# Another stored order of the same tasks in a one-core attention and gated-MLP kernel

## The chip, the cores and the metric

One core of a Trainium2 chip runs the whole program. The metric is the device time of one execution in microseconds (us). Engines are named as in the profile: PE (TensorE; PEld is its weight load), DVE (VectorE), ACT (ScalarE), POOL (GpSimd), SP (SyncE, which issues all DMAs here).

## The reference

For 8 batches of 576 positions, 8 heads of 64 each:

```python
q_d, k_d, v_d = means of q, k, v over groups of 4 positions
out_d = softmax(q_d k_d^T / 8) v_d                  # 144 positions, repeated 4 times
out_l = softmax(q k^T / 8, only |i-j| < 4) v        # a band of 7
x = out_up + out_l                                  # heads side by side: 576 x 512
h = gelu_tanh(x @ w_in)                             # 512 -> 1024
u, v = halves of h; v_n = layernorm(v) * g_ln
gated = u * (w_sg @ v_n + b_sg)                     # w_sg: 576 x 576 over positions
return x + gated @ w_out
```

## The kernel before, in words

Heads are worked on in pairs: 8 batches of 4 pairs give g = 0 to 31. Everything is cut into 2,432 named tasks of one to some thirty instructions. For a pair g: `lq`, `lk`, `lv`, `lw` load it (SP); `qs`, `ks`, `vs` sum groups of four positions; `S` and `Y` are the scores of the band and of the pooled keys (PE; one task `YS` from g = 4 on); `mx`, `my` take row maxima, `ia`, `ib` subtract them (g under 4), `ma`, `mb` add the mask instead (g from 4); `ea`, `eb`, `ec` are the exponentials (ACT), `es`, `re`, `rc` the sums and reciprocals, `np`, `nq` the normalizations; `T`, `U`, `t` turn the probabilities on PE, `pa`, `pb`, `pc`, `pe` copy them out of PSUM; `D` multiplies with v (PE); `oe`, `od`, `xa`, `xb` merge both outputs into x.

For a batch b, `v b.s` (5 blocks of positions) and `u b.i` are the two halves of x @ w_in, with GELU in `vg`, `ua` and the layer norm in `vb`, `vp`, `vn`; `s` multiplies with w_sg, `o` with w_out, `oa` adds the result to x, and `os` stores it. From batch 1 on, matrices are split into a high and a low part and multiplied in three passes (`vh`, `vl`, `gh`, `gl` split; from batch 1 or 2 on, `s` and `o` use seven products in place of eight, whose sums are `fa` to `fd` and `ga` to `gd`). In batch 0, `v` is cut finer: `vk s.k` needs x of pair k alone (s is the block of positions) and one block of weights, y k. The weights come as 64-bit words: `w` loads, `wq`, `wu`, `wb`, `wt` make a float of the two words (`wt`, on POOL, comes last), `wh`, `wl` split it.

The order is written out: the string `ORDER` (line 91) holds all tasks in one row, some with an engine behind a slash (`/V` DVE, `/A` ACT, `/P` POOL; without one, the first engine that the task's `add` names). `place` (line 68) reads it: it gives each task its buffers, first freed first used, out of 8 PSUM banks (`ps`), 10 tiles `X` and 38 tiles `R`. The main loop emits tasks in this row, so each engine's queue is the row cut down to its own tasks, and an engine starts a task only after the one ahead of it in its queue. In front of `S0` and `S3`, PE runs 28 and 20 matmuls on zeros (line 1471). SP has at most 6 loads under way (`DEPTH`).

The lines that are spoken of: 608 (`ks`, `qs` on DVE), 611 and 612 (the same on POOL), 674 (`mx`), 713 (`ia`, `ib`), 686 and 688 (`my`), 720 (`es`), 737 (`rc`), 733 (`re` on DVE), 652 (`ma`, `mb`), 418 and 420 (`wb`), 428 (`wt`), 740 and 748 (`np`, `nq` on POOL), 751 and 760 (`T`, `U`, `t`), 812 and 828 (`D`), 665 and 644 (`Y`, `S`), 795, 799 and 835 (`oe`, `od`, `xa`, `xb`), 936 (`vk`, `v` of batch 0), 1250 and 1262 (`ga` to `gd`, `gl`), 1279 (`o`), 1286 (`oa`).

```python
    for word in ORDER.split():
        name, _, e = word.partition("/")
        t = named.pop(name)
        for k in t.takes:
            where[k] = free[k[0]].pop(0)
```

Of the kernel before, what the change touches and what calls it, by code (L numbers as in the profile page):

```python
# [92 lines left out]
qs2/P wuy0 rc0 np0 ib1 S2 mx2 Y2 my2 ea1 ia2 lq3 lk3 ny1 S3 ec1 qs3/P es1 re1 ks3/P nq0/A rc1 np1 ib2 ea2 lq4 qs4/P wy2
lv0 T0 wqy2 ks4 t0 wby0 pa0 U0 Y3 mx3 ia3 ny2 ec2 pb0/V es2 nq1 U1 pc0 pe0 lw0 ib3 ea3 T1 my3 t1 pa1 pb1/V pc1 wty0
re2/V rc2 nq2 ny3/V es3 ec3 pe1 D0 t2 wby2 wz0 oe0 od0 re3 lw1 np2 YS4 wuy2 wty2 wuz0 rc3 nq3 xa0 ma4 mb4 xb0 wy1 wuy1
wqy1 mx4 lv1 T2 np3 U2 pa2 pb2/V lv2 D1 lk5 why2 wby1 nx4 eb4 wty1 lq5 wqz0/V U3 T3 pc2 pe2/V my4 oe1 od1 xa1 xb1 vk0.0
vk2.0 why0 ks5 qs5 vs2 pa3 ny4 pb3 ec4 wly0 vk2.1 wz3 pc3 t3 wbz0 YS5 my5 ma5 mb5 wly2 ea4 wuz3 vk0.1 wtz0 wqz3 vk1.0
re4 rc4 np4 ny5 ec5 lw2 D2 mx5 oe2/V whz0 od2 lv3 xa2 vs3 vk3.0 vk3.1 xb2 nx5 wbz3 wtz3 wy3 pe3 wqy3/V wby3 eb5 ea5
vk1.1 vk1.2 T4 wuy3 re5/V rc5 lw3 D3 vk0.2 nq4/A oe3/V U4 wty3 od3 xa3 xb3 lv4 vk2.2 vs4/V v0.0 nq5 np5 pa4 whz3 vg0.0
v0.2 vg0.2 why3 v0.1 lw4 vg0.1 lq6 qs6 pb4/V pc4/V wz1 wqz1/V wbz1 wlz3 t4 pe4 wz2 wuz2 vb0.2/A vk3.2 wly3 lk6 wq0 ks6/P  # L100
vb0.0 vp0.0 wlz0 T5 v0.3 pa5 vg0.3 wuz1 wtz1 wqz2/V wbz2 D4 YS6 ma6 my6 U5 pb5/V pc5/V mb6 mx6 wtz2 wq2 whq2 vk4.0 vk4.1
u0.4 nx6/V oe4 vb0.1/A vp0.1 lw5 whq0 vn0.0 vp0.2 u0.5 whz1 ny6 wlq2/V vn0.1 vh0.1/V wq4 eb6 ec6 vb0.3 lq7 od4 ea6 re6
ua0.4 ua0.5 whq4/V xa4 wr1 vk4.2 v0.4 t5 xb4 vg0.4 qs7 wr2 wqr2/V u0.2 ua0.2 vl0.1/P u0.6 pe5 vn0.2 vh0.0 wlz1 why1
vp0.3 vn0.3 u0.3 ua0.6 rc6 np6 T6 wqr1/V wur2 ua0.3 wlq0 lv5 vs5/V small vh0.3 lk7 wq3 whq3 wbr2 ks7 wlq4 wbr1 D5 lw7
pa6 YS7 nq6 U6 oe5/V lv6 od5 xa5 my7 ma7 lk8 ks8 vs6/V wur1 mb7 vb0.4/A xb5 pb6 ny7 ec7 u0.0 ua0.0 wly1 vl0.0/P vp0.4
mx7 pc6/V wq1 whq1/V vn0.4 lq8 wlq3/V wlq1/V u0.1 lw6 t6 pe6 lk9 ua0.1 vl0.3/P vh0.2 b u0.7 ua0.7 vh0.4/V vl0.2 nx7 eb7
D6 qs8/P YS8 lk10 ea7 ma8 mb8 my8 ny8 mx8 oe6 nx8/V eb8 lq9 ec8 vl0.4/P s0.0 sa0.0 xh5/V s0.2 ks9/P re7/V sm0.0 rc7
np7/V nq7 ea8 re8 s0.1 wtr2 s0.3 lv7 U7 T7 t7 vs7/V sa0.1 sm0.1/P s0.5 od6 xa6 sa0.2 sm0.2/P sa0.3 pa7 pb7 pc7 pe7/V D7
gh0.0/A rc8 xb6 xh6 qs9 YS9 sm0.3/P sa0.5 whz2 oe7/V np8 T8 s0.4 nq8/A whr2 wr0 wur0 wr3 wtr1 wur3 od7 xa7 ma9 mb9 xb7
xh7 sm0.5/P pa8 U8 pb8 gh0.1/A my9 mx9 t8 lq10 ny9 lv8 vs8/V tq1 pc8 ec9 pe8/V ks10 xl6/P whr1/V s0.7 sa0.7 xh4 nx9  # L110
sa0.4 ea9 qs10/P lw8 D8 oe8 wlz2 YS10 ma10 mb10 eb9 re9 my10 xl7 lk11 xl4/P xc4 od8 xl5/P gl0.1 s0.6 tq3 v1.0 sm0.7/P
ks11 wqr0 wqr3/V rc9 nq9 ny10/V ec10 np9/V vg1.0 vb1.0/A xc7/A v1.3 v1.2 T9 lv9 vs9/V xa8 sm0.4/P t9 xb8 gl0.0/V sa0.6
gh0.2 wbr3 U9 lq11 qs11/P xc5 sm0.6/P gh0.3/A vg1.3 pa9 gl0.2 pb9/V pc9 pe9/V wtr3 xc6/A mx10 tq2 nx10 tq4 v1.1 lw9
vg1.1 wlr1 wbr0 vg1.2 D9 YS11 tq0 ma11 wtr0 vp1.0 vb1.1/A mb11 my11 mx11 u1.2 whr3 wlr3/V gl0.3/V vb1.2/A whr0 lk12
vn1.0/A vb1.3/A u1.0 ua1.0 wlr2/V ua1.2 lq12 nx11 vp1.3 ks12/P oe9/V od9 xa9 u1.4 xb9 lv10 wlr0/V eb10 ta1/V ta2/V
vs10/V sg vp1.1 gi vp1.2 ta4/V eb11 qs12/P o0.4 oa0.4 o0.6 oa0.6 th2 tl2/V v1.4 o0.5 ta5 o0.0 oa0.0 ea10 re10 vn1.1/A
oa0.5 o0.1 br bd/P ny11 ec11 o0.7 th5/V rc10 nq10/A vn1.2/A tl5 oa0.1 os0.2 ta3/V zf3 vn1.3 np10/V vh1.3/V va1.4/V vj1.4
th4 xh9 oa0.7 lq13 ea11 o0.3 o0.2 vh1.0 u1.3 bea vl1.3/P beb/P U10 vl1.0 oa0.2 vh1.2 vl1.2/P ua1.4 re11/V t10 T10 pa10
vh1.1/V tl4/V pb10 u1.1 u1.7 bec u1.5 pc10 pe10/V ua1.1 gt vl1.1 os0.3 vg1.4 vb1.4/A vp1.4 zf0/V ua1.5 ua1.7 oa0.3
vn1.4/A bed ua1.3 vh1.4 rc11 np11 lw10 D10 lv11 YS12 lq14 gs oe10/V od10 T11 u1.6 qs13/P xa10 vl1.4/P xb10 xh10 xh8 ma12  # L120
my12 ua1.6 s1.1 lk13 zf1 lw12 nq11/A t11 mb12 U11 mx12 s1.0 xl8 nx12/V ea12 pa11 pb11/V sa1.1 sm1.1 zs1 pc11 vs11 pe11
ks13 s1.2 lw11 lk14 sa1.0 ny12 D11 ec12 sm1.0 zf2/V YS13 sa1.2 eb12 re12 oe11/V ks14/P s1.3 my13 ny13 xl10/P xc8/A rc12
nq12/A s1.4 ma13 xl9/P zh1 mb13 mx13 nx13 ea13 xc10/A s1.5 np12 lv12 s1.7 sa1.3 s1.6 od11 xa11 xc9/A xb11 qs14 sm1.3/P
sa1.5 T12 zs3 sm1.2 sa1.4 vs12/V xh11 ec13 eb13 re13 th1 sm1.5/P sa1.7 sm1.7 xl11/P U12 pa12 pb12 pc12 gh1.0/A t12 rc13
u2.0 pe12 D12 YS14 lq16 lw14 zs2/V zs4/V bsa sm1.4 sa1.6 sm1.6 lv13 ga1/V nq13/A gb1 bsb bsc oe12/V my14 ny14/V v2.3
ma14 mb14 gh1.3/A os0.0 mx14 gl1.0 ec14 nx14 ea14 eb14 zl1 ua2.0 v2.0 gl1.3/V o1.15 gh1.4 gd1/V lq15 qs15 v2.1 vg2.1
gl1.4/V zh2/V zl2 th3 o1.05 vs13/V od12 xa12 o1.01 oa1.05 o1.11 zh4 gc1 vg2.3 gh1.2 oa1.10 tl1/V oa1.00 v2.2 o1.06 lk15
np13/V gh1.1/A zl4/V gl1.1/V ks15 vg2.0 xb12 o1.12 oa1.14 o1.16 vb2.0/A xc11 gl1.2 vb2.1/A re14 vg2.2 oa1.15 T13 pa13
t13 U13 pb13 bsd o1.03 oa1.11 lw13 oa1.01 o1.13 oa1.06 pc13 vp2.1 gh1.5/A zh3 pe13/V oa1.16 D13 YS15 lw15 zl3/V gl1.5/V
oe13/V ma15 xh12 tl3 gh1.6/A vb2.2/A vp2.0 vn2.0/A mb15 o1.17 gl1.6 my15 v2.4 od13 ny15/V lk16 o1.07 lv14 os1.1 mx15  # L130
rc14 nx15/V ec15 u2.2 eb15 vp2.2 nq14 vb2.3 oa1.12 o1.14 xa13 oa1.02 va2.4/V np14 U14 vn2.2/A vj2.4 oa1.13 T14 os0.1
vp2.3 vn2.1/A ks16 t14 o1.04 os1.3 vn2.3 fa2/V fh2.1/V pa14 qs16 o1.02 oa1.04 os1.0 vs14 pb14 pc14 u2.4 lk17 pe14 oa1.03
xb13 u2.1 fc2.1 ua2.2 vh2.1 fc2.0 vh2.3/V ua2.4 os1.2 vg2.4 vh2.0 D14 lw16 lv15 ea15 YS16 fb2/V fh2.2 vb2.4 ma16 mb16
u2.5 oe14/V od14 lq17 vl2.3/P vl2.1/P xa14 xb14 u2.3 re15 rc15 vl2.0/P xh13 my16 fd2 nq15/A mx16 u2.7 fl2.1/V vp2.4
vn2.4 vc2/V ny16 ec16 fl2.2/V ua2.5 ua2.7 u2.6 vh2.2/V vl2.2/P vh2.4 s2.05 s2.15 ua2.1 ua2.3 nx16 ua2.6 s2.11 sx2.10
s2.01 sx2.00 np15/V T15 vs15/V U15 pa15/V pb15/V pc15/V t15 pe15/V s2.16 xh14/V s2.06 lk18 D15 lv16 eb16 sx2.01/V
sx2.12/V fh2.4 sx2.11/V qs17 oe15 od15 xa15 vl2.4/P s2.12 sy2.10 xb15 s2.17 sy2.12 ea16 re16/V s2.02 fl2.4 sy2.00 rc16
nq16/A s2.07 s2.13 ks17/P xl14 sx2.02 sy2.11 ks18 lq18 YS17 lq19 np16 ma17 mb17 lk19 sy2.02 t16 s2.14 T16 my17 xh15 xl15
sa2.0 ny17 xl12 sa2.2 s2.04 U16 xl13/P pa16 pb16/V ec17 gh2.0/A pc16 sa2.3 qs18/P pe16 sa2.6 mx17 s2.03 vs16/V v3.0
sy2.01 sa2.1/V ga2/V sa2.7/V vg3.0 nx17 ea17 D16 oe16 YS18 lv17 lk20 sa2.5/V gb2 gc2 my18 sa2.4 gd2 ny18/V v3.2 gh2.2/A  # L140
gl2.0/V v3.1 od16 xa16 eb17 re17 vb3.0 lw18 ma18 mb18 o2.11 o2.01 oa2.10 gh2.3/A ec18 gh2.1 gh2.4/A xc14/A gl2.3 vg3.2
vb3.2/A oa2.00 xc12/A gl2.4 mx18 vp3.0 nx18/V gl2.2/V gl2.1/V o2.15 oa2.15 o2.05 v3.3 vp3.2 rc17 nq17 xc13/A xb16 o2.16
oa2.05 oa2.11 o2.13 xc15/A o2.06 o2.03 lw17 oa2.16 gh2.6 gl2.6 gh2.5/A gl2.5 v3.4 o2.02 ea18 lq20 eb18 re18 vs17/V vn3.2
oa2.06 vg3.1 vb3.1/A u3.5 np17 oa2.04 o2.17 va3.4/V oa2.01 o2.07 vg3.3 vn3.0 vb3.3/A ks19/P qs20 t17 T17 oa2.12 rc18
nq18/A os2.0 oa2.02 U17 o2.14 o2.04 pa17 pb17 vp3.1 vn3.1 pc17 pe17 qs19/P ua3.5 vj3.4 vg3.4 u3.4 oa2.13 o2.12 vp3.3
vn3.3/A oa2.03 np18/V D17 YS19 lv18 vh3.3 oa2.14 os2.1 fa3/V fc3.1 oe17 ua3.4 od17 xa17 my19 t18 os2.2 u3.7 ma19 mb19
# [1393 lines left out]
```

## Time and profile before

| | us |
|---|---|
| median of 3 runs | 546.87 (546.45 to 547.45) |
| the profiled execution, its own time | 547.18 |
| its span, first to last instruction | 545.4 |
| PE busy in the span | 538.2 (99%) |
| DVE, ACT, POOL busy | 459.0 (84%), 424.5 (78%), 352.6 (65%) |

The span lies 1.8 us under that execution's own time, and that execution 0.31 us over the median. PE's busy time counts each matmul from issue to its modelled end. The granted clock was 1.00 in all 40 slices of the span but the last (0.99).

### The profile page before, as it was taken

The numbers are of one execution on the slowest core, as the hardware profiler recorded it, in microseconds if no ns is written. First come the engines' busy times: TensorE is split into PE (matmuls) and PEld (weight loads), VectorE is DVE, ScalarE is ACT, GpSimd is POOL, SyncE is SP. The second block draws the span as 40 slices with busy tenths as digits, with TensorE's granted clock in tenths as the row PEclk, the third lists the DMA queues.
The fourth block names the chain that finished last, engine by engine and source line by source line (L and its number), as shares of the span: only waits on it lengthen the run. The fifth ranks groups of instructions, "written<-read, shape, count | busy, mean of one in ns | idle before, by whom it ended". The sixth has DMA issues, their size and how long they took to land.

```text
span 545.4 us, 17291 instructions
## 1 busy us (share of the span) xinstructions
PE 538.2 (99%) x6737; PEld 492.1 (90%) x6737; DVE 459.0 (84%) x993; ACT 424.5 (78%) x1427; POOL 352.6 (65%) x418
## 2 busy tenths in 40 slices
...
GB/s 305 233 300 331 116 220 141 147 101 95 158 35 128 70 186 123 118 71 80 46 128 132 116 146 93 115 47 82 106 142 105 27 146 102 60 0 1 65 2 109
DMA packets 31841, 64.47 MB, mean 118 GB/s; under 512 B 3728, under 2 KB 4752, under 8 KB 31760
## 3 DMA queue, kind: packets, MB, share of 16 engines
...
q14 instruction: 28, 0.23, 0.1%
...
## 4 chain that ended last, share of the span: by engine, by line
PE 95%; DVE 3%; ACT 2%; issue 0%; ACTq 0%
PE ps L1144 24%; PE ps L943 17%; PE ps L1098 15%; PE ps L1279 15%; PE ps L936 3%; PE ps L812 3%; PE ps L644 3%; PE ps L828 3%; PE ps L751 3%; PE ps L1155 3%; PE ps L760 3%; PE ps L665 3%; PE ps L1471 1%; DVE stats L674 1%; DVE X L713 1%; DVE sums L720 0%
## 5 line engine op out<-in xcount | busy, mean ns | idle before, releaser
L1144 PE MATMUL ps<-X,weight_z 128*128 128x288 f32 x448 | 94.7, 297 | 0.0
L704 ACT ACTIVATE X<-X,nb 128x64 f32<-128x64 f32 x280 | 93.7, 340 | 1.2 <-DVE nb L683 0.8
L943 PE MATMUL ps<-weight_y,X 128*128 128x512 f32 x280 | 84.5, 395 | 0.0
L1144 PEld LDWEIGHTS ps<-X,weight_z 128*128 128x128 f32 x448 | 73.4, 188 | 0.3
L1144 PE MATMUL ps<-R,weight_z 128*128 128x288 f32 x224 | 65.9, 294 | 0.0
L1286 DVE TENSOR_TENSOR R<-ps,R 128x288 f32<-128x288 f32 x98 | 42.5, 450 | 22.3 <-PE ps L1279 21.7
L943 PEld LDWEIGHTS ps<-weight_y,X 128*128 128x128 f32 x280 | 51.4, 188 | 10.7
L247 ACT CAST R<-R 128x576 fp32r<-128x576 f32 (+2 forms) x73 | 46.4, 648 | 14.8 <-DVE R L1250 8.0
L1033 POOL TENSOR_TENSOR R<-R,R 128x512 fp32r<-128x512 f32 (+1 forms) x23 | 30.7, 1341 | 36.4 <-DVE R L247 14.7
L704 ACT ACTIVATION_READ_ACCUMULATOR X<-X,nb 128x1 f32 x280 | 53.6, 191 | 0.0
L1279 PE MATMUL ps<-R,weight_r 128*128 128x288 f32 x336 | 50.1, 296 | 0.0
L1098 PE MATMUL ps<-wsg_h,R 128*128 128x288 f32 x228 | 49.7, 299 | 0.0
L1262 POOL TENSOR_TENSOR R<-R,R 128x576 fp32r<-128x576 f32 x25 | 38.5, 1554 | 14.7 <-DVE R L484 4.9
L1279 PEld LDWEIGHTS ps<-R,weight_r 128*128 128x128 f32 x336 | 46.6, 188 | 1.1
L943 PE MATMUL ps<-weight_y,R 128*128 128x512 f32 x112 | 44.2, 395 | 0.0
L247 ACT COPY R<-ps 128x464 f32<-128x464 f32 (+4 forms) x92 | 32.8, 394 | 13.8 <-PE ps L760 4.7
L1144 PEld LDWEIGHTS ps<-R,weight_z 128*128 128x128 f32 x224 | 42.2, 188 | 0.1
L1279 PE MATMUL ps<-R,R 128*128 128x288 f32 x252 | 38.0, 298 | 0.0
L1098 PEld LDWEIGHTS ps<-wsg_h,R 128*128 128x128 f32 x228 | 37.4, 188 | 0.4 <-DVE R L1033 0.3
L726 ACT ACTIVATE pd<-ps,nbd 128x144 f32<-128x144 f32 x96 | 35.4, 378 | 2.5 <-PE ps L943 1.6
L1279 PEld LDWEIGHTS ps<-R,R 128*128 128x128 f32 x252 | 34.7, 188 | 0.6
L1250 POOL TENSOR_TENSOR R<-R,R 128x576 f32<-128x576 f32 x14 | 23.3, 1668 | 16.4 <-DVE R L1250 6.1
...
## 6 DMA issues: line engine op xcount, KB each, us to landing
...
```

The lines of the kernel that those rows point to most:

```text
L247: (nc.scalar.copy if e == "A" else ENG[e].tensor_copy)(**kw)
L644: nc.tensor.matmul(out=sp[i][os, c * KB:(c + 1) * KB], lhsT=q[hs, t * QB:t * QB + KB], rhs=k[hs, t * QB:t * QB + KB], start=not early, sto ...
L704: nc.scalar.activation(out=st["ms"][:, t, :], in_=src, func=AF.Exp, bias=st["nb"][:, t:t + 1], scale=scale, accum_out=sums[par][:, t:t + 1])
L726: nc.scalar.activation(out=pd[:, n], in_=st["sdv"][n].rearrange("p (c k) -> p c k", c=3), func=AF.Exp, bias=st["nbd"][:, n:n + 1], scale=s ...
L943: nc.tensor.matmul(out=acc, lhsT=r32(l), rhs=r32(weights[f"y{k}"][:, 0, w]), start=(i == 0 and ks[0] == 0), stop=(i == len(ops) - 1 and ks ...
L1033: ENG[e].tensor_tensor(out=r32(dst), in0=vact[s][0][0:n], in1=vh[0:n, 0:DM], op=ALU.subtract)
L1098: nc.tensor.matmul(out=s_bank(j, c), lhsT=r32(l), rhs=r32(r), start=first_in and i == 0, stop=i == len(ops) - 1, skip_group_check=not firs ...
L1144: nc.tensor.matmul(out=acc[:, 0:HALF], lhsT=r32(l), rhs=r32(r), start=(first and n == 0), stop=(last and n == len(ops) - 1))
L1250: ENG[e].tensor_tensor(out=us[out], in0=us[a], in1=us[c], op=ALU.subtract)
L1262: ENG[e].tensor_tensor(out=r32(gl[m]), in0=us[raws[m]], in1=gh[m], op=ALU.subtract)
L1279: nc.tensor.matmul(out=bank(j, c), lhsT=r32(l), rhs=r32(r), start=first and i == 0, stop=i == len(ops) - 1, skip_group_check=not first)
L1286: nc.vector.tensor_tensor(out=x, in0=bank(j, c), in1=x, op=ALU.add)
```

## The change

`ORDER` holds the same 2,432 names in another row, and 433 of them on another engine; no other line differs. On each engine the counts stay close: PE has the same 490 tasks, DVE 864 tasks where it had 860, ACT 600 where it had 604, POOL 289 as before. The table of functions that ACT loads changes 42 times in both.

```diff
 ORDER = """
-lk0 lq0 qs0/P ks0 lk1 ks1 lq1 qs1/P S0 mx0 ia0 ib0 S1 mx1 lk4 lk2 ea0 Y0 my0 ny0 Y1 lq2 ks2 ec0 es0 re0 ia1 wy0 wqy0 my1
...
+lq1 qs1 lq0 lk0 lk1 S0 mx0 ks0/P S1 qs0/P wy2 ia0 ib0 Y0 ks1/P Y1 ea0 lk2 lk3 mx1 my0 my1 ks2/P lq2 qs2/P es0 ia1 ks3/P
...
```

The first place is the start of POOL's queue, from its first sums to its second normalization (`half` is a scratch tile, `kd` and `qd` hold the summed k and q, `X` the probabilities). Before:

```order
L611 TENSOR_TENSOR half<-R_166 128x288
L612 TENSOR_TENSOR qd_89<-half 128x144
L611 TENSOR_TENSOR half<-R_175 128x288
L612 TENSOR_TENSOR qd_90<-half 128x144
L611 TENSOR_TENSOR half<-R_292 128x288
L612 TENSOR_TENSOR qd_89<-half 128x144
L740 TENSOR_TENSOR X_235<-X_235,rc_108 128x640
L611 TENSOR_TENSOR half<-R_355 128x288
L612 TENSOR_TENSOR qd_90<-half 128x144
L611 TENSOR_TENSOR half<-R_357 128x288
L612 TENSOR_TENSOR kd_98<-half 128x144
L740 TENSOR_TENSOR X_300<-X_300,rc_109 128x640
```

The last part of the same stretch in the change, behind three sums (`ks0`, `qs0`, `ks1`) of the same form:

```order
L611 TENSOR_TENSOR half<-R_287 128x288
L612 TENSOR_TENSOR kd_97<-half 128x144
L611 TENSOR_TENSOR half<-R_300 128x288
L612 TENSOR_TENSOR qd_89<-half 128x144
L611 TENSOR_TENSOR half<-R_289 128x288
L612 TENSOR_TENSOR kd_98<-half 128x144
L611 TENSOR_TENSOR half<-R_313 128x288
L612 TENSOR_TENSOR qd_90<-half 128x144
L740 TENSOR_TENSOR X_260<-X_260,rc_108 128x640
L740 TENSOR_TENSOR X_306<-X_306,rc_109 128x640
```

Seven sums stand ahead of the first normalization where three stood; `ks0`, `ks1`, `ks2` and `ks4` came to POOL from DVE, and `qs1` went the other way.

The second place is DVE's queue around the merge of pair 0 into x (`xa0` and `xb0`, the two L835; `rc3` is the L737, `ma4` and `mb4` the two L652, `oe0` the L795, `od0` the L799). Before:

```order
L420 SCALAR_TENSOR_TENSOR R_573<-weight_y_428,ps_572 128x512
L799 SCALAR_TENSOR_TENSOR od_91<-ps_516,da 128x288
L737 RECIPROCAL rc_109<-sums_96 128x13
L835 TENSOR_TENSOR R_621<-ps_515,od_91 128x5x58
L652 TENSOR_TENSOR X_623<-ps_594,mask_sb 128x256
L652 TENSOR_TENSOR X_623<-ps_595,mask_sb 128x384
L835 TENSOR_TENSOR R_621<-ps_516,od_91 128x5x58
```

In the change:

```order
L720 TENSOR_REDUCE sums_96<-X_466 128x10
L795 TENSOR_SCALAR da<-ps_528 128x144
L799 SCALAR_TENSOR_TENSOR od_91<-ps_529,da 128x288
L835 TENSOR_TENSOR R_638<-ps_528,od_91 128x5x58
L835 TENSOR_TENSOR R_638<-ps_529,od_91 128x5x58
L737 RECIPROCAL rc_109<-sums_96 128x13
L652 TENSOR_TENSOR X_711<-ps_602,mask_sb 128x256
L652 TENSOR_TENSOR X_711<-ps_603,mask_sb 128x384
```

`oe0` came to DVE from ACT; `rc3`, `ma4` and `mb4` moved behind the merge.

The third place is PE's queue around the first matmuls of batch 0 (L936; `vk0.0`, `vk2.0`, then the pieces of the next pair). Before, the turns of pair 3 (`U3` and `T3`: the first L751, the L760, the second L751) stand ahead of them:

```order
L751 MATMUL ps_729<-turn_l,X_469 128x122
L760 MATMUL ps_729<-turn_p,pd_102 112x112 x3
L751 MATMUL ps_734<-turn_l,X_469 128x122 x4
L936 MATMUL ps_749<-R_447,R_621 128x512
L936 MATMUL ps_751<-R_447,R_621 128x512
L936 MATMUL ps_751<-R_715,R_746 128x512
L760 MATMUL ps_776<-turn_p,pd_102 112x112 x2
```

In the change `U2` stands ahead, and `T3` and `U3` follow behind `vk0.0` and `vk2.0`:

```order
L751 MATMUL ps_726<-turn_l,X_431 128x122
L760 MATMUL ps_726<-turn_p,pd_101 112x112 x3
L936 MATMUL ps_731<-R_446,R_638 128x512
L936 MATMUL ps_733<-R_446,R_638 128x512
L751 MATMUL ps_750<-turn_l,X_466 128x122 x4
L751 MATMUL ps_767<-turn_l,X_466 128x122
L760 MATMUL ps_767<-turn_p,pd_102 112x112 x3
L936 MATMUL ps_731<-R_722,R_740 128x512
L936 MATMUL ps_733<-R_722,R_740 128x512
```

The first two `vk` moved ahead of the turns of pair 3. At the other end, both orders close with `o7.13 oa7.06 os7.0.1 oa7.16 os7.1.1`.

## Rows read from the trace of the kernel before

**Rows 1.** The page, part 1: busy time of the engines, share of the span, instructions.
```profile
PE 538.2 (99%) x6737; PEld 492.1 (90%) x6737; DVE 459.0 (84%) x993; ACT 424.5 (78%) x1427; POOL 352.6 (65%) x418
```

**Rows 2.** Waits of PE: waiter, releaser, us in total, times, longest.
```profile
PE ps L665 <- DVE R L420: 1.0, 1, 1.0
...
PE ps L751 <- DVE X L713: 0.4, 1, 0.4
PE ps L760 <- ACT pd L745: 0.3, 1, 0.3
```

**Rows 3.** PE's timeline: start, us, what [idle before <- releaser].
```profile
1.04 5.53 PE L1471 MATMUL ps<-zeros 128*128 128x256 bf16 x28 [1.04 <-DVE mask_sb L311]
...
12.03 0.84 PE L665 MATMUL ps<-kd,qd 64*64 64x144 f32 x16 [0.66 <-ACT pd L726]
12.80 2.36 PE L1471 MATMUL ps<-zeros 128*128 128x256 bf16 x20
...
29.03 0.32 PE L751 MATMUL ps<-turn_l,X 122*128 122x122 f32 x1
...
30.50 2.84 PE L936 MATMUL ps<-R,R 128*128 128x512 f32 x6 [0.44 <-ACT R L247]
...
36.75 0.64 PE L812 MATMUL ps<-R,vd 48*64 48x144 f32 x15
```

**Rows 4.** The chain that ended last, its last two pieces: start, us, what.
```profile
530.89 11.36 PE ps L1279 x84
...
542.27 0.46 DVE R L1286
```

**Rows 5.** DVE's timeline in the first 27 us.
```profile
6.10 0.75 DVE L608 TENSOR_REDUCE kd<-R 128x144 f32<-128x576 f32 x1 [1.64 <-DMA R<-in_kT_dram]
...
10.74 0.74 DVE L608 TENSOR_REDUCE kd<-R 128x144 f32<-128x576 f32 x1
11.40 0.81 DVE L720 TENSOR_REDUCE sums<-X 128x10 f32<-128x640 f32 x1
12.13 0.41 DVE L713 TENSOR_TENSOR X<-ps,stats 128x256 f32<-128x256 f32 x1
12.46 0.45 DVE L686 TENSOR_REDUCE stats<-ps 128x2 f32<-128x288 f32 x1
...
13.18 0.49 DVE L713 TENSOR_TENSOR X<-ps,stats 128x384 f32<-128x384 f32 x1
...
25.61 0.88 DVE L652 TENSOR_TENSOR X<-ps,mask_sb 128x256 f32<-128x256 f32 x2
26.40 0.45 DVE L835 TENSOR_TENSOR R<-ps,od 128x290 f32<-128x290 f32 x1
```

**Rows 6.** POOL's timeline in the first 22 us.
```profile
7.64 0.67 POOL L611 TENSOR_TENSOR half<-R 128x288 f32<-128x288 f32 x1 [1.94 <-DMA R<-in_qT_dram]
...
9.78 0.67 POOL L611 TENSOR_TENSOR half<-R 128x288 f32<-128x288 f32 x1 [0.96 <-DMA R<-in_qT_dram]
...
13.34 1.26 POOL L740 TENSOR_TENSOR X<-X,rc 128x640 f32<-128x640 f32 x1 [2.39 <-DVE rc L737]
15.81 0.67 POOL L611 TENSOR_TENSOR half<-R 128x288 f32<-128x288 f32 x1
...
16.94 1.26 POOL L740 TENSOR_TENSOR X<-X,rc 128x640 f32<-128x640 f32 x1
...
20.16 1.30 POOL L428 TENSOR_TENSOR R<-R,weight_y 128x512 int32<-128x512 int32 x1
```

**Rows 7.** POOL's timeline near the end.
```profile
528.02 2.00 POOL L1250 TENSOR_TENSOR R<-R,R 128x576 f32<-128x576 f32 x1
...
533.26 5.69 POOL L1262 TENSOR_TENSOR R<-R,R 128x576 fp32r<-128x576 f32 x4 [1.31 <-ACT R L247]
```

**Rows 8.** DVE's timeline near the end.
```profile
528.65 1.98 DVE L1262 TENSOR_TENSOR R<-R,R 128x576 fp32r<-128x576 f32 x1
...
532.00 0.76 DVE L1250 TENSOR_TENSOR R<-R,R 128x576 f32<-128x576 f32 x1
```

More of the change, by code (lines that the diff above doesn't have):

```diff
@@ L91 @@
 ORDER = """
-lk0 lq0 qs0/P ks0 lk1 ks1 lq1 qs1/P S0 mx0 ia0 ib0 S1 mx1 lk4 lk2 ea0 Y0 my0 ny0 Y1 lq2 ks2 ec0 es0 re0 ia1 wy0 wqy0 my1
[L93 to L146, printed above, removed]
```

176 lines of the change are left out of this document (115 added, 61 removed).

## The prediction, made before the change was run

> **What bounds the kernel now.** Read the page first, then what PE waits for, then PE's timeline, then the end of the chain. The page says that PE is busy 538.2 of 545.4 us [rows 1]. That leaves 7.2 us, and the change gives PE the same tasks, so idle time of PE is all that an order can win. PE waits six times in all; three of the waits stand in [rows 2], the other three as brackets in [rows 3]. They are 1.04 at the start, 0.66 at 12.03, 0.3 ahead of a turn (L760), 1.0 ahead of pooled scores (L665), 0.4 ahead of a turn (L751) and 0.44 at 30.50, together 3.8 us. So from 30.50 on PE never waits, until its last matmul; the chain ends with 84 matmuls in 11.36 us and one DVE add at 542.27 [rows 4]. The rest of the idle time is the end: that add and the last store, 545.4 - 542.3 = 3.1 us.
>
> What the reader is to see: 500 us in the middle can only get worse, and what can be won lies ahead of 30.50. There PE does small attention tasks and waits for DVE, ACT and POOL; from `vk0.0` (L936) on it has large matmuls of batch 0 to fill in.
>
> **The change part by part.** *The start.* The 28 matmuls on zeros run from 1.04 to 6.57 [rows 3] in both orders, and the first scores need the first three loads. The third load has landed by 6.10 [rows 5], so the new order of the loads costs the first scores nothing. The fourth lands by 7.64 and the seventh by 9.78 [rows 6]: 0.71 us a load of 293 KB. In the change a weight of 512 KB comes fifth (estimate from those 0.71 us: 1.25) and `lq2` eighth, so it lands at 7.64 + 1.25 + 3 x 0.71 = 11.0. `S2` waits for it and is over near 12.3, but the task behind it waits for something later still.
>
> *A wait added.* That task is `Y2`. It takes the PSUM banks that `ia1` and `ib1` free, and these are now behind `my1` and `es0` on DVE. DVE reaches 10.74 as before (there `ks2` started) [rows 5]. Then come `my1`, some 0.6 (0.37 for the L686 row, its 0.45 less the 0.08 by which neighbours overlap, and some 0.2 for the L688 half as wide), `es0` 0.73 (11.40 to 12.13), `ia1` 0.33 (12.13 to 12.46) and `ib1` 0.41 (0.49 less 0.08) [rows 5]: 12.8. `Y2` ran at 12.03 before [rows 3], so it is some 0.77 us late, and behind it queue the 20 matmuls on zeros and `S3`.
>
> *The sums moved to POOL.* Four sums of k leave DVE and one of q comes to it. On POOL a sum takes 1.13 (15.81 to 16.94), a normalization 1.26 [rows 6]. Three sums go from 6.10 to 9.5, `ks2` follows its load, `qs2` starts with its load at 11.0, then `ks3` and `qs3`: `np0` starts at 14.4, 1.06 after the 13.34 of before, and `np1` at 15.65, 1.3 earlier than 16.94 [rows 6]. `T0` needs `np0` at 15.65. PE gets there later than that (the zeros at 12.80 + 0.77 = 13.57, 2.36 for them [rows 3], some 1.2 for `S3`: 17.1), so the longer queue is hidden by PE's own work. If that cover went, each late normalization would hold the turn behind it. Then follow `nq1`, one sum and `wt` of the first weight, which starts at 18.9 where it started at 20.16 [rows 6].
>
> *What leaves DVE.* Ahead of the merge of pair 0, `ks2` and `ks4` go (0.66 each, 10.74 to 11.40), `ma4` and `mb4` move behind it (0.79, 25.61 to 26.40) [rows 5], and small ones go (`pb0`, `ny3`, `rc3`, some 0.4); `re1` and `oe0` come (some 0.4). That is 2.1 us less: `xb0`, which started at 26.40, ends at some 24.6 in place of 26.8.
>
> *PE up to `vk0.0`.* From the start of the 20 matmuls on zeros at 12.80 to 30.50 are 17.70 us [rows 3]. In them lie four waits of 2.1 us (0.3, 1.0, 0.4, 0.44) and `U3` and `T3`, which the change puts behind `vk0.0`: from 29.03 to the last wait's start at 30.06, 1.0 us. If none of the four waits is left, `vk0.0` starts at 13.57 + 17.70 - 2.1 - 1.0 = 28.2. `D1` is the tightest on the way: it needs the banks that `xa0` and `xb0` free at 24.6, and PE comes to it at about 24.7. PE is then 30.50 - 28.2 - 1.0 = 1.3 us ahead of before.
>
> Two things lie on either side of this. Idle time understates a wait: the matmul ahead of it also drains, and the one behind it fills, so up to 0.25 us each for four waits is won besides (the L751 row is 0.32 long [rows 3]): 2.3. And small delays in a queue of this length can take back a few tenths. I take the middle, **1.8 us**.
>
> *Behind `vk0.0`.* `vk0.1` needs the second weight from POOL. Ahead of it stand, from 18.9 on, three `wt` of 1.30 (itself among them) and a `wl` like them, two `np` of 1.26, one sum of 1.13 [rows 6] and two `nq` of some 0.85 (432 of the 640 columns of an `np`): 10.6 us, so it ends at 29.5. PE arrives at 28.2 + 2 x 0.95 (2.84 / 3) [rows 3] + 1.0 = 31.1. That covers it by 1.6 us. `v0.2` needs the fourth weight, which by the same count ends at some 41. PE reaches `v0.2` behind twelve `vk` (11.4 us) and the attention tasks among them, some 5 us by the length of those in [rows 3]: at about 45.
>
> *The middle and the end.* From there to 542 nothing can be won. 433 tasks change engine, but the counts per engine stay (DVE + 4, ACT - 4). I cost this at nothing, covered by PE's own matmuls. At the end both orders close with the same five tasks, so the 3.1 us stay. Near it `o7.06` has less cover: four tasks of PE (0.81 each, 11.36 / 14 [rows 4]) stand between `s7.14` and it, and in that time `sa7.6`, `gd7` on DVE and `gl7.4` on POOL must run: 0.46 [rows 4], 0.68 (0.76 less 0.08) [rows 8] and 1.42 (5.69 / 4) [rows 7] = 2.6 of 3.2. If POOL's takes 2.00 [rows 7] and the DVE one 1.98 [rows 8], as one of each did, it is 4.4: a price of 0 to 1.2, and 0 taken, since one row in five was slow.
>
> **The sum.** 545.4 - 1.8 = 543.6 of span, and 547.2 - 1.8 = 545.4 for the profiled execution. The median stands 0.3 lower, so **545.1 us**. Bounds: 0 won, if the waits only change place, and 2.8 if all five waits after the first go and nothing is added: 544.1.
>
> **The rivals.**
>
> *The waits change place.* `Y2` is the pattern: an order that packs other work in front of a task makes it wait elsewhere. For it speaks that DVE, ACT and POOL are all close to full in this stretch (DVE's rows from 10.74 on show no gap [rows 5]). A slip of 1 us at `D1` or at `T0` and the gain is under 0.8. Time: 546.0 to 547.5, 546.7 taken.
>
> *All five waits go, and drains with them.* Then `Y2` would have to run at 12.03, against the count above. 544.1 or a little less.
>
> *POOL becomes the bound (slower).* Between `np0` at 14.4 and the fourth weight at 41 POOL has 27 us of work nearly without a break. Near the end one POOL subtraction took 2.00 us, and four like it later 1.42 each [rows 7]; while the slow one ran, a DVE subtraction of two SBUF operands took 1.98, where the like took 0.76 at 532.00 [rows 8]. If two thirds of the 27 us were stretched by 2.00 / 1.42 = 1.4, the fourth weight would come 7.2 us later, at 48.2, and PE, there at 45, would wait 3.2 us: 545.1 + 3.2 = 548.3. It costs from a delay of 4 us on, and from 5.8 the change is slower than before. Against it: in the first 22 us POOL's instructions take the same time in each row (0.67 thrice, 1.26 twice) [rows 6], while DVE runs beside them mainly reductions with one operand and subtractions that read PSUM [rows 5].
> [...]
>
> *A wait in the middle.* Somewhere behind 45 us a producer comes late, where today none does. Each microsecond late is a microsecond of time. Without a place to name it gets a small chance: 547.5 and up.
>
> *The order changes what PE does.* The same matmuls in another row can switch between shapes more or less often. Moves between attention and large tasks are 209 where they were 216, so this is some tenths either way, and lies inside the range.
>
> **How the numbers follow.** A measurement of this kernel can tell about 0.2%, 1.1 us, from no change: faster means under 545.8. The forecast (1.2 to 2.4 won) has 0.55, waits that change place 0.22, all waits gone 0.08, POOL 0.07, a wait in the middle 0.08. Faster: 0.55 + 0.08, and 0.01 of the second: 0.64. Same: most of the second, 0.20, and small losses in the middle, 0.03: 0.23. Slower: 0.13. The range runs from 543.8 (all waits gone, with the spread of a median) to 547.3 and leaves out the case of POOL and most of the waits in the middle.
>
> **What would show it.** In the changed profile: `Y2` (L665) released by DVE near 12.8; the first L936 near 28 with L751 behind its first two; few or no waits of PE between 13 and 30; the first `D` on pooled v (L812 with `vd`), at 36.75 before [rows 3], with one `vk` less ahead of it near 34.5; 3.1 us from the last matmul to the end. The prediction is wrong if PE shows waits behind 30 us, if POOL's rows in 14 to 42 us are longer than in rows 6, or if the first L936 starts after 29.

## The result and the profile after

The change takes 549.58 us (median of 5 runs, 549.31 to 551.31) where the kernel before takes 546.87 (546.45 to 547.49): a ratio of 1.0054, 95% interval 1.0037 to 1.0072, 2.7 us **slower**. Forecast were 545.1 us and a range that ended at 547.3. The profiled execution of the change is the one of 551.31 (span 549.5); the spans of the other four are 547.5 to 548.1. A second profile of the same kernel (549.88, span 548.1, below) tells what is there each time.

The page and the waits of PE, to be held against [rows 1] and [rows 2]:

```profile
PE 539.9 (98%) x6737; PEld 493.2 (90%) x6737; DVE 464.8 (85%) x993; ACT 419.2 (76%) x1420; POOL 341.5 (62%) x414
...
PE ps L1279 <- DVE R L1286: 1.6, 1, 1.6
PE ps L1471 <- DVE mask_sb L311: 1.0, 1, 1.0
PE ps L665 <- ACT R L247: 0.8, 1, 0.8
PE ps L812 <- issue: 0.7, 1, 0.7
PE ps L665 <- DVE X L713: 0.7, 1, 0.7
PE ps L665 <- POOL kd L612: 0.5, 1, 0.5
PE ps L760 <- POOL pd L748: 0.4, 1, 0.4
PE ps L828 <- issue: 0.3, 1, 0.3
PE ps L1098 <- DVE R L1065: 0.2, 1, 0.2
```

PE waits 6.2 us instead of 3.8. The longest wait is new, and is where the prediction had none: an output product (L1279) waits 1.6 us for an eviction of VectorE (L1286; an eviction moves a result out of a PSUM bank, so that the bank can be filled again), twelve microseconds before the end. Its place in the timelines of VectorE, GpSimd (POOL) and PE, as in [rows 7, 8]:

```profile
533.00 0.52 DVE L1132 SCALAR_TENSOR_TENSOR R<-ps,g_sb,R 128x288 f32<-128x288 f32 x1 [0.44 <-PE ps L1098]
533.55 1.98 DVE L1250 TENSOR_TENSOR R<-R,R 128x576 f32<-128x576 f32 x1
535.56 1.55 DVE L247 CAST R<-R 128x576 fp32r<-128x576 f32 x1
537.03 0.44 DVE L1286 TENSOR_TENSOR R<-ps,R 128x288 f32<-128x288 f32 x1
537.40 1.82 DVE L1262 TENSOR_TENSOR R<-R,R 128x576 fp32r<-128x576 f32 x1
...
541.91 0.45 DVE L247 CAST R<-R 128x576 fp32r<-128x576 f32 x1
...
533.48 3.31 POOL L1262 TENSOR_TENSOR R<-R,R 128x576 fp32r<-128x576 f32 x2 [2.58 <-ACT R L247]
537.19 1.42 POOL L1262 TENSOR_TENSOR R<-R,R 128x576 fp32r<-128x576 f32 x1 [0.40 <-DVE R L247]
...
537.62 1.03 PE L1279 MATMUL ps<-R,R 128*128 128x288 f32 x6 [1.55 <-DVE R L1286]
```

In tasks: `sa7.6`, `gd7`, `gh7.6`, `oa7.00`, `gl7.1` on VectorE; `gl7.4` and `gl7.5`, then `gl7.6` on GpSimd; `o7.06` on PE, which needs the bank that `oa7.00` frees. `gd7` took 0.76 before [rows 8], here 1.98; the cast takes 0.45 at 541.91, here 1.55. GpSimd's first subtraction starts 0.07 us ahead of `gd7`, and its two are over at 536.79, and the cast ends 0.3 behind them. So VectorE stands behind GpSimd for 2.3 us, just where an eviction is queued that PE needs.

**Where the time goes.** The table lays the traces over each other at equal work of PE (the matmuls done so far, each at the usual spacing of its kind): by how many us the change is behind the kernel before (a negative number: ahead of it). It is worked out from the starts of all matmuls.

| us of PE's work done | 14 | 40 | 60 | 200 | 220 | 400 | 420 | 510 | 520 | 528 | 530 | 532 | end |
|---|---|---|---|---|---|---|---|---|---|---|---|---|---|
| first profile | 1.65 | 0.57 | 0.43 | 0.80 | 1.33 | 1.46 | 1.96 | 2.38 | 2.00 | 2.01 | 3.81 | 4.29 | 4.06 |
| second profile | 1.21 | -0.80 | -0.95 | -0.60 | -0.06 | 0.07 | 0.50 | 0.93 | 0.54 | 0.55 | 2.37 | 2.85 | 2.64 |

The head wins 0.95 in the second profile; in the first its third load landed late (the first sum on GpSimd, which waits for it, starts at 7.10, in the second at 6.05) and it loses 0.4. Then both fall back in the same steps: some 0.5 at 213 us (PE's time; 212.94 in the first profile, 211.55 in the second), 0.4 to 0.5 at 419, 0.3 to 0.4 near 500 (0.4 is won back near 520), and 2.1 at the end.

Held against the forecast, which had the change 1.8 ahead, the second profile is 4.4 us late: 0.85 in the head (to 60 us), 1.5 in the middle (60 to 528), 2.1 at the end.

### The profile page after: what moved, and what is told of

It reads as the page before. It is cut to its first block, busy times and chain, and to the rows that moved or that the text cites. A ratio compares the mean times of both kernels' runs of the same rounds, so it can differ in the third digit from the quotient of the medians.

```text
span 549.5 us, 17272 instructions
## 1 busy us (share of the span) xinstructions
PE 539.9 (98%) x6737; PEld 493.2 (90%) x6737; DVE 464.8 (85%) x993; ACT 419.2 (76%) x1420; POOL 341.5 (62%) x414
## 4 chain that ended last, share of the span: by engine, by line
PE 89%; DVE 4%; ACT 3%; issue 1%; DVEq 0%; ACTq 0%
PE ps L1144 22%; PE ps L943 16%; PE ps L1098 15%; PE ps L1279 12%; PE ps L812 3%; PE ps L936 3%; PE ps L751 3%; PE ps L828 3%; PE ps L1155 3%; PE ps L644 3%; PE ps L760 3%; PE ps L665 2%; ACT X L704 1%; ACT R L247 1%; DVE R L1286 0%
## 5 line engine op out<-in xcount | busy, mean ns | idle before, releaser
L1286 DVE TENSOR_TENSOR R<-ps,R 128x288 f32<-128x288 f32 x98 | 42.5, 449 | 17.6 <-PE ps L1279 17.2
L1279 PE MATMUL ps<-R,weight_r 128*128 128x288 f32 x336 | 50.9, 297 | 0.1
L1098 PE MATMUL ps<-wsg_h,R 128*128 128x288 f32 x228 | 49.5, 298 | 0.2 <-DVE R L1065 0.2
L1279 PEld LDWEIGHTS ps<-R,weight_r 128*128 128x128 f32 x336 | 46.7, 188 | 1.3 <-DVE R L1262 0.3
L740 POOL TENSOR_TENSOR X<-X,rc 128x640 f32<-128x640 f32 x25 | 32.9, 1318 | 17.8 <-DVE rc L737 17.2
L247 ACT COPY R<-ps 128x464 f32<-128x464 f32 (+4 forms) x96 | 34.0, 394 | 11.9 <-PE ps L751 5.6
L1033 POOL TENSOR_TENSOR R<-R,R 128x512 fp32r<-128x512 f32 (+1 forms) x18 | 23.8, 1326 | 25.5 <-ACT R L247 7.6
L1279 PE MATMUL ps<-R,R 128*128 128x288 f32 x252 | 38.0, 298 | 1.6 <-DVE R L1286 1.6
L1098 PEld LDWEIGHTS ps<-wsg_h,R 128*128 128x128 f32 x228 | 37.5, 188 | 0.4 <-DVE R L1065 0.4
L1279 PEld LDWEIGHTS ps<-R,R 128*128 128x128 f32 x252 | 35.0, 188 | 2.9 <-issue 1.8
```

The costliest lines, as they stand in the source:

```text
L247: (nc.scalar.copy if e == "A" else ENG[e].tensor_copy)(**kw)
L740: ENG[e].tensor_tensor(out=st["ms"], in0=st["ms"], in1=bc_last(st["rc"][:, 0:NT], KB), op=ALU.mult)
L1033: ENG[e].tensor_tensor(out=r32(dst), in0=vact[s][0][0:n], in1=vh[0:n, 0:DM], op=ALU.subtract)
L1098: nc.tensor.matmul(out=s_bank(j, c), lhsT=r32(l), rhs=r32(r), start=first_in and i == 0, stop=i == len(ops) - 1, skip_group_check=not firs ...
L1279: nc.tensor.matmul(out=bank(j, c), lhsT=r32(l), rhs=r32(r), start=first and i == 0, stop=i == len(ops) - 1, skip_group_check=not first)
L1286: nc.vector.tensor_tensor(out=x, in0=bank(j, c), in1=x, op=ALU.add)
```

## Experiments

All edits are of the order alone. Theory E: the loss is the end, by VectorE and GpSimd holding each other (a row is held when it is long because the other engine's row runs beside it). Theory H: the head. Theory M: the middle.

### Head, middle and end apart

```diff
 e1_head:   ORDER = change up to its 383rd task, then the rest as in before
 e2_end:    ORDER = before up to its 2215th task, then the rest as in the change
 e3_middle: ORDER = before up to its 389th task, then the change, from 479 us on before
 e4_after:  ORDER = change
```

> Head alone: the changed order up to its 383rd task (through YS8, about the first 78 us), then the order of before with the tasks that are left. Theory H (the new first loads and sums delay PE's start, and the head costs more than the trace of the change says): 1.5 us or more above the kernel before, 548.4 to 549.5. Theory E (the loss is in the last ten microseconds): the head is about even, 546.9 to 547.6 (the trace of the change stands 0.5 us behind from 42 us on). My prediction on record would have it at 545.1, 1.8 below.

> End alone: the order of before up to its 2215th task (about 479 us), then the tasks that are left in the changed order. Theory E (VectorE is held on the way to the first output eviction of the last block by GpSimd's subtractions beside it): 1.4 to 2.0 us above before, 548.3 to 548.9, and a wait of PE of about 1.5 us some 10 us before the end. Theory H: within 0.3 us of before.

> Middle alone: the order of before up to about 78 us, the changed order from there to about 479 us, and then the order of before for the tasks that are left. If the rows of the two traces hold for the timed runs, 0.3 to 0.8 us above before (547.2 to 547.7): the trace of the change falls behind by 0.5 us at 200 to 220 us and wins some of it back later. A theory M, by which buffers freed in another order cost more in the middle than one trace shows, expects 1.5 us or more above before.

> The changed kernel once more, unaltered: 549.0 to 550.0. Its trace shows which waits are there in every execution: by theory E the wait of 1.5 us for the first output eviction of the last block is there again, and the sum of the three parts run apart (head, middle, end, each against before) gives its loss of 2.7 us within 0.5 us. If the wait is gone in this trace and the time is still 549.6, theory E falls.

Measured, beside before at 547.30: head 547.09 (ratio 0.9993, 0.9978 to 1.0008), end 548.95 (1.0034, 1.0013 to 1.0055), middle 546.65 (0.9993, 0.9976 to 1.0011), the change 549.60 (1.0038, 1.0023 to 1.0054). The end alone is slower, the others are not, and the wait is there again in both kernels that have it; here the change, second profile:

```profile
532.10 1.98 DVE L1250 TENSOR_TENSOR R<-R,R 128x576 f32<-128x576 f32 x1
534.11 1.55 DVE L247 CAST R<-R 128x576 fp32r<-128x576 f32 x1
535.58 0.45 DVE L1286 TENSOR_TENSOR R<-ps,R 128x288 f32<-128x288 f32 x1
...
532.03 3.31 POOL L1262 TENSOR_TENSOR R<-R,R 128x576 fp32r<-128x576 f32 x2 [2.58 <-ACT R L247]
...
536.17 1.03 PE L1279 MATMUL ps<-R,R 128*128 128x288 f32 x6 [1.55 <-DVE R L1286]
```

Theories H and M, as they were put, fall. What I expected of the sum does too: the parts give -0.2 - 0.65 + 1.65 = +0.8, the whole +2.3. Either the intervals (0.8 to 1.2 us each way) hold the gap, or head and middle cost more together than apart; run `g4_no_end` asks that. (The middle alone also came out below its forecast of 547.2 to 547.7. And the head alone is not quite that: its profile is 0.95 ahead at 60 us of PE's work and 0.2 at 100, behind the seam where the order of before takes over.)

### The end: a cast moved, a tie turned, a neighbour taken away

```diff
 g1_cast_on_act
-... sa7.6 gd7/V gh7.6 o7.05 o7.01 gh7.5/A gh7.4/A o7.15 oa7.00 gh7.1/A gl7.1/V ...
+... sa7.6 gd7/V o7.05 o7.01 gh7.5/A gh7.4/A o7.15 oa7.00 gh7.1/A gh7.6/A gl7.1/V ...
 g2_tie_turned
-... gh7.5/A gh7.4/A o7.15 oa7.00 gh7.1/A gl7.1/V ...
+... gh7.5/A gh7.1/A o7.15 oa7.00 gh7.4/A gl7.1/V ...
 g3_pool_off
-... oa7.00 gh7.1/A gl7.1/V o7.11 oa7.10 oa7.15 gl7.4 o7.06 o7.12 o7.16 oa7.01 gl7.5 ...
+... oa7.00 gl7.4/V gh7.1/A gl7.1/V o7.11 oa7.10 oa7.15 gl7.5/V o7.06 o7.12 o7.16 oa7.01 ...
 g4_no_end: ORDER = change up to its 2218th task, then the rest as in before
```

> The changed order with one cast of the last block (gh7.6) on ScalarE instead of VectorE, behind ScalarE's other three casts. In the trace of the change VectorE runs 1.98 us (gd7) and 1.55 us (gh7.6) ahead of the eviction oa7.00 for which PE waits 1.55 us. Theory E: oa7.00 starts when gd7 ends, PE's wait falls from 1.55 to 0.4 us or less, and 1.1 to 1.5 us are won: 548.1 to 548.5 where the change has 549.6. Theory N (it is the number of tasks ahead of the eviction, at their normal 0.76 and 0.45 us): 0.45 us won, 549.1.

> The changed order with two casts of the last block swapped on ScalarE (gh7.1 ahead of gh7.4), so that GpSimd's subtraction gl7.4 can start only 0.65 us later, and VectorE's gd7, which started 0.07 us behind it, starts first. Theory E (whichever of the two engines starts first holds the other): gd7 takes 0.76 instead of 1.98 us, GpSimd's subtraction is the longer one, and PE's wait is 0 (gh7.6 at 0.45) to 0.6 us (gh7.6 held behind gl7.4): 548.1 to 548.7. A rival, by which these subtractions are slow on VectorE whenever GpSimd subtracts beside them, whoever starts first: gd7 stays near 1.98 us and the wait near 1.5: 549.6.

> The changed order with the two subtractions gl7.4 and gl7.5 on VectorE (behind oa7.00 and behind oa7.15) instead of GpSimd, so that GpSimd does nothing beside gd7 and gh7.6. Theory E: gd7 0.76 and gh7.6 0.45 us, oa7.00 is 2.3 us earlier, PE's wait for it is gone, and what is left is at most 0.5 us for gl7.4 on VectorE: 548.0 to 548.6. The rival, that these rows are long by themselves in this place (their operands, not their neighbour): both stay long, gl7.4's 0.7 us comes on top, and the time is 550.2 or more.

> The changed order up to its 2218th task (about 479 us), then the order of before for the tasks that are left: the change without its end. If the parts add up as they were timed alone (head 0.2 below before, middle 0.65 below), 546.4. If the trace of the whole change is right (it is 0.8 us ahead at 60 us, and waits at 213, 419 and 503 us that the middle alone does not show take that back and 0.9 more), 547.7 to 548.0, and then these waits depend on the head that comes before them.

Measured, beside before at 547.39: `g1_cast_on_act` 547.68 (1.0003, 0.9988 to 1.0018), `g2_tie_turned` 547.42 (0.9996, 0.9982 to 1.0010), `g3_pool_off` 548.89 (1.0024, 1.0009 to 1.0038), `g4_no_end` 547.35 (0.9993, 0.9980 to 1.0007). **Two casts of ScalarE swapped take away the whole 2.3 us** by which the change stood above before. The first two won more than forecast (548.1 to 548.5 and 548.1 to 548.7; theory N's 549.1 is out too): with PE's wait goes what it loses behind it. VectorE, GpSimd and PE at that place in `g2_tie_turned`:

```profile
531.60 0.76 DVE L1250 TENSOR_TENSOR R<-R,R 128x576 f32<-128x576 f32 x1
532.40 0.46 DVE L247 CAST R<-R 128x576 fp32r<-128x576 f32 x1
532.77 0.45 DVE L1286 TENSOR_TENSOR R<-ps,R 128x288 f32<-128x288 f32 x1
533.14 1.84 DVE L1262 TENSOR_TENSOR R<-R,R 128x576 fp32r<-128x576 f32 x1
...
532.93 4.73 POOL L1262 TENSOR_TENSOR R<-R,R 128x576 fp32r<-128x576 f32 x3 [3.98 <-ACT R L247]
...
533.97 0.99 PE L1279 MATMUL ps<-R,R 128*128 128x288 f32 x6
```

The swap moved GpSimd's start from 0.07 us ahead of `gd7` to 1.33 behind it; `gd7` and the cast have their short times back, and PE's row has no bracket. (The next subtraction, `gl7.1`, is now the one that loses, 1.84, and nobody waits for it.) That is more than a turned tie: GpSimd starts only after the cast has ended (532.86), so this run shows that the neighbour costs the time, and not yet that who starts first decides. The rival, slow beside GpSimd whoever starts first, falls by rows of the kernel before. There VectorE's subtraction starts 0.04 us ahead of the GpSimd row of 2.00 in [rows 7] and is short, that row is long (1.42 to 1.45 where free), and the rows that start behind it, on either engine, are long in turn (VectorE's 1.98 in [rows 8] is the one between these two):

```profile
527.98 0.76 DVE L1250 TENSOR_TENSOR R<-R,R 128x576 f32<-128x576 f32 x1 [0.97 <-POOL R L1135]
...
529.99 1.96 POOL L1262 TENSOR_TENSOR R<-R,R 128x576 fp32r<-128x576 f32 x1
```

The 14 profiles have 168 subtractions of this shape on VectorE, both operands in SBUF, that took over 0.9 us. Each started while a row of GpSimd ran, and ended 0.61 to 0.62 us behind that row's end. The 135 that started ahead of GpSimd's row took 0.69 to 0.76. (One row, in `e1_head`, started 0.20 us behind by the records and took 0.74; there GpSimd's took 2.96.) In `g1_cast_on_act` `gd7` is still long, 1.97, but the eviction follows it at once, so what PE waits for is on time: the length of a held row costs only what is queued behind it.

`g3_pool_off` has `gd7` at 0.76 and the cast at 0.46 with no subtraction of GpSimd beside them, as theory E says, and against its rival. Its time misses what I expected, because the hold only moved: `gl7.4`, now on VectorE, and `gl7.1` behind it take 2.52 for two (1.42 where free) beside GpSimd's `gl7.6`, and PE waits for the first (0.38) and for an eviction behind them (0.32):

```profile
533.17 2.52 DVE L1262 TENSOR_TENSOR R<-R,R 128x576 fp32r<-128x576 f32 x2
...
532.96 1.43 POOL L1262 TENSOR_TENSOR R<-R,R 128x576 fp32r<-128x576 f32 x1 [3.98 <-DVE R L247]
...
535.07 0.53 PE L1279 MATMUL ps<-R,R 128*128 128x288 f32 x2 [0.38 <-DVE R L1262]
...
537.50 1.86 PE L1279 MATMUL ps<-R,R 128*128 128x288 f32 x12 [0.32 <-DVE R L1286]
```

`g4_no_end`, without the end, stands at before's time: between the 546.4 of the parts and the 547.7 of the trace, and its interval (546.3 to 547.8) can't tell these apart. In its trace what the head wins (1.2 us at 60 us of PE's work) the middle takes back (0.1 is left at 420).

### The middle's tie and the head's wait

At 213 us stands the same thing in small. In the change `fl2.1` (VectorE, L1065) starts 0.03 us behind GpSimd's `vl2.2` (L1033); in `e3_middle`, also 0.03 behind by the records, it wins. First the change, second profile, then `e3_middle` (whose lines are numbered 4 lower):

```profile
209.70 1.79 DVE L1065 TENSOR_TENSOR R<-R,R 128x512 fp32r<-128x512 f32 x1
...
209.67 1.27 POOL L1033 TENSOR_TENSOR R<-R,R 128x512 fp32r<-128x512 f32 x1 [2.45 <-ACT pd L726]
...
211.55 0.40 PE L1098 MATMUL ps<-wsg_h,R 128*128 128x288 f32 x1 [0.17 <-DVE R L1065]
```

```profile
209.79 0.69 DVE L1061 TENSOR_TENSOR R<-R,R 128x512 fp32r<-128x512 f32 x1
...
209.76 1.86 POOL L1029 TENSOR_TENSOR R<-R,R 128x512 fp32r<-128x512 f32 x1 [2.46 <-ACT pd L722]
```

One of the two is 0.6 to 1.1 us longer, never both. (So what I wrote ahead of the run on `fl2.1`, that it had been ahead in `e3_middle`, is not what the rows show: the order of starts 0.03 us apart can't be read from them.) The edits, on top of `g2_tie_turned` for the first three and of `g4_no_end` for the last:

```diff
 h1_fl_first (also in h3_both, h4_both_end)
-... np15/V s2.11 ua2.4 fl2.1/V s2.15 ...
+... fl2.1/V np15/V s2.11 ua2.4 s2.15 ...
 h2_head (also in h3_both, h4_both_end)
-... pa1 pb1/V re2/V Y3 my3 ny3 wz0 t1 wuy2 ... np2 ea3 pc1 pe1 D0 ... YS4 ec3 es3 re3 why0 lk5 t2 oe0/V od0 xa0 xb0 ...
+... pa1 pb1/V pc1 re2/V Y3 my3 ny3 wz0 t1 pe1 wuy2 ... np2 ea3 D0 ... YS4 ec3 why0 lk5 t2 oe0/V od0 xa0 xb0 es3 re3 ...
```

> The changed order with the two casts of the last block swapped (as in the run before that won 2.2 us), and with VectorE's subtraction fl2.1 placed ahead of its np15 instead of behind it. In the trace of the change fl2.1 started 0.03 us behind a subtraction of GpSimd (209.70 and 209.67), took 1.79 us, and PE fell back by 0.5 to 0.7 us at 213 us; in the run of the middle alone it was ahead, took 0.69 us, and PE lost nothing. Theory E (who starts first) expects fl2.1 at 0.69 us, no wait of PE at 213 us, and 0.5 us less than with the casts alone: 546.9. If the loss at 213 us has another cause: 547.4, with PE's wait for fl2.1 still there.

> The changed order with the two casts of the last block swapped, and with the head mended where PE's longest stable wait of it stands: pc1 and pe1 are evicted on ScalarE right behind pa1 and t1 (not behind ny3 and ea3, which wait for VectorE), and VectorE's es3 and re3 go behind xa0 and xb0. By theory W (the head won less than predicted because of the 0.84 us that YS4 waits for pc1's bank) the wait before YS4 goes, PE's first product with vk stands near 28.4 instead of 29.2, and the time is 0.6 to 0.8 us less than with the casts alone: 546.7. Rival: the next wait (D1 on xb0's bank) takes its place, 547.2 to 547.4.

> The changed order with all three: casts swapped, fl2.1 first, head mended. If both waits are as the theories have them and don't give each other back: 1.1 to 1.4 us less than with the casts alone, 546.1, and below the kernel before by about 1.2 us. If a later wait takes what the head wins: 546.9.

> The changed order up to its 2218th task with fl2.1 first and the head mended, and from there the order of before: 545.9 to 546.3 if head, middle and end add up (547.35 for the change with the end of before, less 1.1 to 1.4), 547.0 if what the head wins is waited for later.

Measured, beside before at 547.17: `h1_fl_first` 547.07 (0.9992, 0.9983 to 1.0001), `h2_head` 547.78 (1.0005, 0.9995 to 1.0015), `h3_both` 547.48 (1.0000, 0.9990 to 1.0009), `h4_both_end` 547.34 (0.9995, 0.9980 to 1.0010). None beats before beyond its interval. `h3_both` and `h4_both_end` missed both of their forecasts (546.1 or 546.9; 545.9 to 546.3 or 547.0), and `h2_head` came out above both of its own.

`h1_fl_first` by its rows does what theory E expects; GpSimd's is now the long one (`np15` starts on VectorE 0.09 ahead of it, at 209.98), and PE's waits have no L1098 any more (at equal work -0.20 at 200, -0.17 at 220, where the change loses 0.54):

```profile
209.38 0.68 DVE L1065 TENSOR_TENSOR R<-R,R 128x512 fp32r<-128x512 f32 x1
...
210.07 1.88 POOL L1033 TENSOR_TENSOR R<-R,R 128x512 fp32r<-128x512 f32 x1 [2.44 <-ACT pd L726]
```

Its time, 0.35 us below the casts alone, can't be told from none; this execution lost 0.4 at 419 us, as the change does. In `h2_head` the wait before `YS4` is gone and another stands behind it, the rival's outcome, though not on the bank that the rival named; in `h3_both` PE waits 0.44 at its first L936, for VectorE (L420). PE in the change (second profile), then in `h2_head`:

```profile
24.33 0.53 PE L665 MATMUL ps<-kd,qd 64*64 64x144 f32 x10 [0.84 <-ACT R L247]
...
29.38 1.90 PE L936 MATMUL ps<-R,R 128*128 128x512 f32 x4
```

```profile
27.07 1.61 PE L812 MATMUL ps<-R,R 48*64 48x144 f32 x54 [1.00 <-issue]
29.88 1.89 PE L936 MATMUL ps<-R,R 128*128 128x512 f32 x4
```

**Near 500 us**, where no run was made, the rows show one more hold. In the second profile PE's product (L1279) comes 0.3 late at 500.21, released by an eviction of VectorE (L1286, from 499.71). In VectorE's queue ahead of it stands a scaling with one operand in SBUF (L1013), which starts 0.57 behind a subtraction of GpSimd. It takes 1.16 there and 0.54 at 500.80:

```profile
498.18 1.16 DVE L1013 TENSOR_SCALAR R<-R,mv,rs 128x512 f32<-128x512 f32 x1
...
500.80 0.54 DVE L1013 TENSOR_SCALAR R<-R,mv,rs 128x512 f32<-128x512 f32 x1
...
497.61 1.44 POOL L1262 TENSOR_TENSOR R<-R,R 128x576 fp32r<-128x576 f32 x1
```

In `e2_end`, where the scaling starts 0.84 behind, it takes 0.89, and PE loses 0.1 at most.

**What "issue" may be.** No task releases these waits. The trace has a queue q8 of kind "instruction" (53 packets of 16 KB in a run: 868 KB, or some 64 bytes for each of PE's 6737 matmuls and 6737 weight loads, so these may be PE's own instructions; no run shows it), and the packet of that stretch comes late where PE stalls. At 419 us, its landing is counted from when PE begins a fixed matmul some 3 us ahead of the stall; in `D1`, from when PE begins the same matmul by count:

| place | landing, us | what PE lost there |
|---|---|---|
| 419 us, 7 profiles | -3.2 to 1.30 | 0.0 in each |
| 419 us, 7 profiles | 1.39, 1.43, 1.61, 1.63, 1.64, 1.66, 1.70 | 0.25, 0.16, 0.25, 0.43, 0.43, 0.44, 0.51 |
| `D1`, 10 profiles | -2.2 to -0.97 | 0.1 at most |
| `D1`, 4 profiles | -0.54, -0.53, -0.15, 0.18 | 0.63, 0.34, 0.88, 1.17 |

Up to 416.3 us, where PE passes that matmul, the change's first profile shows no packet of q8 behind the one of 402, and has it just then; `g2_tie_turned`, whose tasks are the same up to there, already had it. The DMA view of the change's first profile from 403.0 to 416.3 us, from 416.3 to 419.0, and of `g2_tie_turned` from 403.0 to 414.8:

```profile
q1 hardware_dynamic: 989, 2.04, 50.2%
q14 instruction: 1, 0.01, 0.2%
...
q1 hardware_dynamic: 228, 0.40, 48.1%
q8 instruction: 1, 0.02, 2.4%
```

```profile
q1 hardware_dynamic: 868, 1.79, 48.4%
q8 instruction: 1, 0.02, 0.5%
```

That is a relation over 14 profiles. No run moved a packet, and why one comes late is open.

## Why the prediction was wrong

- **The end: the step that failed.** "a price of 0 to 1.2, and 0 taken, since one row in five was slow". The count of the cover was right: 2.6 us of VectorE and GpSimd against 3.2 of PE if nothing is held. The price was taken as a frequency, where it hung on one pair of tasks: `gl7.4` and `gd7` start when ScalarE's casts and `sa7.6` release them, and these come 0.07 us apart in each profile that has this end, GpSimd first. The frequency was miscounted besides: [rows 7] leave out the GpSimd row of 1.96 at 529.99, so two in six were slow, and each slow row of that stretch, on either engine, had started while the other engine's ran. The sum also left out `gh7.6`, the cast between `gd7` and the eviction whose bank `o7.06` needs, and it came long too (1.55). Measured: 1.55 of wait and 0.5 to 0.7 behind it, and 2.2 us won by one swap (549.60 to 547.42).
- **The rival "POOL becomes the bound"** had the mechanism, in the wrong place: in the head GpSimd's rows kept their lengths (0.67, 1.26), and the hold cost time at the end, where [rows 7, 8] showed a pair of it. It also weighed only VectorE's rows with two operands in SBUF as held: the cast has one, and was held too. The Trainium skill, "SBUF — State Buffer", section "Who interferes with whom", says of VectorE's two-port modes that whoever issues first gets the pair of ports shared with GpSimd for the whole instruction while the other fully blocks; that a cast can enter these modes; and that issue order, not the kind of operation, decides who blocks. The traces agree: 0.76 for the subtraction that starts ahead and 1.98 for the one that starts behind, 1.55 and 0.45 for the cast beside GpSimd's row and without it. By that rule the sum would have had the full 1.2 and more.
- **`Y2`, right.** 12.8 forecast; 13.10 in the second profile, 12.65 to 13.54 in the eleven that have this head.
- **The sums on GpSimd, sized a little low.** A sum with a sum behind it took 1.25 (7.30 to 8.55 in the second profile), not 1.13, which was one with a normalization behind it [rows 6]: `np0` at 15.05, not 14.4. As said, PE's own work hid it, but for 0 to 0.55 at a turn (0.16 in the second profile).
- **The merge of pair 0, wrong by 1.6.** `xb0` ended at 26.2, not 24.6: 0.7 earlier than before and not 2.1. And `YS4` waited 0.84 for a bank that `pc1` frees on ScalarE, behind `ny3`, which waits for VectorE, and two more; I had followed VectorE alone. The first L936 came at 29.38, not 28.2: 0.3 from `Y2`, 0.16 from the turn, 0.84 from `YS4`. The head wins 0.95 us in the second profile (0.6 to 1.3 in the others with the same head, but for the first), not 1.8.
- **The middle, costed at nothing.** A tie lost at 213 us (0.5), the stall at 419 us (0 to 0.5) and 0.3 near 500 us (another hold, by its rows) take back what the head wins. "So from 30.50 on PE never waits" was true of that trace and no margin: ties of 0.03 us decided rows that PE needs at once.
- **Its signs of being wrong.** Two of the three came: waits of PE behind 30 us, and the first L936 after 29. The third did not: GpSimd's rows between 14 and 42 us kept their lengths.
